# Weight tiles of six groups kept on chip for two blocks of a mixture's first expert

## The chip, the core and the metric

The kernel runs on one core of a Trainium2 chip. A core has TensorE (PE, matrix products into PSUM), VectorE (DVE), ScalarE (ACT) and GpSimd (POOL), which work side by side on SBUF, and SyncE (SP), which here only issues transfers, in order. Each engine works through its own list of instructions in a fixed order and waits where a semaphore isn't reached. The metric is the device time of one execution in microseconds (us).

## What is computed

Three layers follow each other. Each of 32 heads has a recurrent state of 40 x 40 over 768 steps; the 3072 rows of 320 that come out of it go through a PReLU layer of width 2048 (the first expert) and then through a gated SiLU layer of width 1536 (the second expert). All in float32:

```python
for t in range(S):                               # 768 steps
    y[:, :, t] = einsum('bhd,bhde->bhe', r, state)
    Sa = einsum('bhde,bhe->bhd', state, a)
    state = state * w[:, :, None, :] - einsum('bhd,bhe->bhde', Sa, b) \
            + einsum('bhd,bhe->bhde', v, k)
x = y as 3072 x 320
h = x @ w_in                                     # 320 x 2048
x = (maximum(h, 0) + alpha * minimum(h, 0)) @ w_out
g = x @ w_gate                                   # 320 x 1536
return (silu(g) * (x @ w_val)) @ w_out2          # 1536 x 320
```

## The kernel before

**Blocks.** Time is cut into 6 stages m = 0 to 5 (`NM`) of 128 steps. A stage gives 4 x 128 = 512 rows, called block m. The first expert works on block m - 1 while the sequence part (`seq`) works on stage m, so block 4 is worked on beside the last stage, and block 5 after the sequence has ended. The second expert follows, block by block.

**Order.** The program is written as generators that `drive` takes in turn. A scheduler then lists each engine's instructions by priority and by when it expects them to be ready, and assigns the tiles their places; where a tile's place is still held, the first instruction that writes it waits. Nothing is reordered at run time.

**Weights.** Products are made of a high and a low part, so each weight exists as a pair. `conv` converts a raw weight tile into such a pair (`narrow` and `split`): three steps on VectorE (L175 to L177), then on ScalarE, GpSimd or VectorE. The raw tiles have two places (`RB`). The tiles of the first expert (two per group, 384 and 320 KB) and of the second expert's groups 0 to 3 (`KEEP`) are converted early and stored to DRAM as `wd`. The second expert's groups 4 to 11 are converted late, straight into their place in `wpool` (`direct`, 24 tiles).

**First expert** (`mlp1`). The 2048 columns are 16 groups f of 128 (`K1`). For each group `fetch` (L219) brings the up tile from `wd`, 8 matmuls (`up_mm`) give u in PSUM, ScalarE and VectorE make the PReLU (L271, L272) and split it into gh and gl (L187, L188), and 8 matmuls with the group's down tile (`down_mm`) add to three accumulators d0 to d2. So a group is 16 matmuls and 2 fetched tiles. The down product of a group comes behind the up product of the next (`DEP`). Every tile is fetched anew for every block:

```python
def fetch(pool, idx, up):                        # L219
    t = pool.tile([128, 768], F32R, tag="w", name="wt")
    ...
    fetched.append(nc.sync.dma_start(out=..., in_=wd[idx, :, 0:n]))
```

The pool has 4 places (`WB`). u has one PSUM place for blocks 0 to 4 (`psu`) and three for block 5 (`psu3`). At a block's end its accumulators are copied out (x1o) and stored.

**Second expert.** `wpool` has 12 places (`K2`) for each of three kinds of tiles: w0 (gate), w1 (value) and w2 (down). The pool is set up when the sequence's pools are closed and takes their memory. Beside block 5 run the loads of groups 0 to 3 from `wd` (`kept`, L910, 12 tiles, tied by `issue_after` to fetches of block 5) and conversions of groups 4 to 11, one at every fourth step of `mlp1`; the rest run in the second expert's first block. There, for each of 12 groups, 16 matmuls give gate pg and value pv, SiLU and product (L960, L962) make g, and 12 matmuls add to four accumulators.

Of the kernel before, what the change touches and what calls it, by code (L numbers as in the profile page):

```python
# [7 lines left out]
F32 = mybir.dt.float32  # L8
F32R = mybir.dt.float32r
# [3 lines left out]
PSUM = bass.MemoryType.PSUM  # L13
# [34 lines left out]
FA = 8  # L48
# [12 lines left out]
C2 = 10  # L61
GPB = 2
DEP = 1
HELD = 0
XB = 2
L = 64
HALF = 32
LOOK = 2
# [3 lines left out]
def kernel(  # L72
# [16 lines left out]
    NM, B, _, D, NP, TB = r.shape  # L89
# [6 lines left out]
    BLK = B * TB  # L96
    NB = NT // BLK
    K1 = DFF // 128
    K2 = DFF2 // 128
# [56 lines left out]
    mark = {}  # L156
# [58 lines left out]
    fetched = []  # L215
    e1p = {}
    XAB = [XAB1]

    def fetch(pool, idx, up):  # L219
        t = pool.tile([128, 768], F32R, tag="w", name="wt")  # L220
        n = 768 if up else 2 * DM
        fetched.append(nc.sync.dma_start(out=t[:, 0:n].bitcast(F32), in_=wd[idx, :, 0:n]))
        return t.rearrange("p (a b) -> p a b", a=6) if up else t

# [9 lines left out]
    def down_mm(ps, q, t, gh, gl, first, last):  # L234
        if q < 2:
            wh, wl = t[:, q * 128:q * 128 + 128], t[:, 256 + q * 128:384 + q * 128]
            nc.tensor.matmul(ps, wh, gh, start=first, stop=False)
            nc.tensor.matmul(ps, wh, gl, start=False, stop=False)  # L238
            nc.tensor.matmul(ps, wl, gh, start=False, stop=last)  # L239
        else:  # L240
            both = t[:, 512:2 * DM]
            nc.tensor.matmul(ps, both, gh, start=first, stop=False)
            nc.tensor.matmul(ps, both, gl, start=False, stop=last)
# [48 lines left out]
                conv(stage, 2 * K1 + 3 * f + j, src, f, kind)  # L292
                yield

    def mlp1(j, psu, early=0):
        psd, xp1, gp1, wp1 = (e1p[k] for k in ("psd", "xp", "gp", "wp"))
        half = B // 2 * TB
        xs = new_x(xp1, BLK)
        plan = [(f, 0, half) for f in range(early)] + [(f, half, BLK) for f in range(early)]
        plan += [(f, 0, BLK) for f in range(early, K1)]  # L300
        dps = [psd.tile([128, BLK], F32, tag=f"d{q}", name=f"d{q}") for q in range(3)]
        pend = []

        def down(f, c0, c1, gh, gl):
            t = fetch(wp1, 2 * f + 1, False)
            for q in range(3):
                down_mm(dps[q][:, c0:c1], q, t, gh, gl, f == 0 and c0 == 0, f == K1 - 1)

        seen = set()
        for f, c0, c1 in plan:  # L310
            if not seen & {(c0, c1), (0, half) if early and c0 == 0 else (c0, c1)}:
                with lifted():
                    b0, b1 = c0 // TB, c1 // TB
                    fill_x(xp1, xs, xd[j][:, b0:b1].rearrange("f b t -> f (b t)"), c0, c1)
                seen.add((c0, c1))
                yield
            t = fetch(wp1, 2 * f, True)
            ps = psu.tile([128, c1 - c0], F32, tag="u", name="u")
            up_mm(ps, t, tuple(x[..., c0:c1] for x in xs))
            yield  # L320
            if len(pend) == DEP:
                down(*pend.pop(0))
            pend.append((f, c0, c1, *prelu(gp1, ps, f, c1 - c0)))
            yield
        for e in pend:
            down(*e)
        for q in range(3):
            tc.cur_priority -= XPRI
            o = xp1.tile([128, BLK], F32, tag="xa", name="x1o", bufs=XAB[0])
            if q < 2:  # L330
                nc.scalar.copy(out=o, in_=dps[q])
                nc.sync.dma_start(out=x1d[j][q * 128:q * 128 + 128], in_=o)
            else:
                nc.scalar.copy(out=o[lo], in_=dps[2][hi])
                nc.vector.tensor_tensor(out=o[lo], in0=dps[2][lo], in1=o[lo], op=ALU.add)
                mark["x1"] = nc.sync.dma_start(out=x1d[j][256:DM], in_=o[lo])
            tc.cur_priority += XPRI
            yield
# [49 lines left out]
    for j, pool in ((0, rawp), (1, bp)):  # L388
        for nm in ("wa", "bk"):
            t = raw[nm, j] = pool.tile([128, 2, NP, TB], F32, name=f"raw_{nm}{j}")  # L390
# [10 lines left out]
    for j in range(2):  # L401
        if j < NVT or BVT:
            t = (pers if j < NVT else bp).tile([128, NP, TB], F32, name=f"raw_vt{j}")
# [16 lines left out]
    for j in range(2):  # L420
        t = pers.tile([128, NG, L], F32, name=f"tt{j}")
        TT.append(t)
    ST = []
    for j in range(B):
        t = pers.tile([128, NP, 64], F32, name=f"ST{j}")
# [366 lines left out]
    c1, c2 = conv1(), conv2()  # L792
# [38 lines left out]
    c1 = after(mark["prep"], c1)  # L831
    p1, c1 = behind(p1), behind(c1)
    drive((inverse(0), N_INV, HP), (take(p1, EP), EP + .1, BP), (take(c1, EC), EC + .1, CP), lead=1, engs=G0, lag=LG0, who=W0)
    p1, c1 = after(mark["inv"], p1), after(mark["inv"], c1)
# [16 lines left out]
    ps1 = ctx.enter_context(ExitStack())  # L851
    e1 = ctx.enter_context(ExitStack())
    e1p["psd"] = ps1.enter_context(tc.tile_pool(name="psd1", bufs=1, space=PSUM, side="right"))
    psu = ps1.enter_context(tc.tile_pool(name="psu1", bufs=1, space=PSUM, side="right"))
    e1p["xp"] = e1.enter_context(tc.tile_pool(name="xp1", bufs=1, side="right"))
    e1p["gp"] = e1.enter_context(tc.tile_pool(name="gp1", bufs=GPB, side="right"))
    e1p["wp"] = e1.enter_context(tc.tile_pool(name="wp1", bufs=WB, side="right"))
    gms = [mlp1(j, psu, FA if j == 0 else 0) for j in range(NM - 1)]
    if FA:
        drive(  # L860
            (seq(2, 0), N_SEQ, SP), (seq(3, 1), N_SEQ, SP),
# [3 lines left out]
    for m in range(1, NM):  # L865
        s0_ = m * B
        g = [
            (chain(seq(s0_, 0), seq(s0_ + 2, 0)), 2 * N_SEQ, SQ),
            (chain(seq(s0_ + 1, 1), seq(s0_ + 3, 1)), 2 * N_SEQ, SQ),
        ]  # L870
        if m + 1 < NM:
            g.append((chain(preps(range((m + 1) * B, (m + 2) * B)), lift(inverse(m + 1), PV)), FAC * (B * N_PREP + N_INV), HP))
        gm = gms[m - 1]
        nm = N_MLP + (1 if FA and m == 1 else 0)
        held = HELD if m + 1 == NM else 0
        g.append((take(gm, nm - held), nm, 0))
        if not CG:
            g.append((take(c2, CS[m - 1]), CS[m - 1], 0))
        drive(*g, lead=2, engs=G2, lag=LG2, who=W2)
        if CG:  # L880
            for _ in take(after(mark["inv"], c2), CS[m - 1]):
                pass
        assert m + 1 == NM or next(gm, 0) == 0
    ap_.close()
    at.close()
    pa.close()
    cv.close()
    with tc.issue_after(mark["seq"].ins):
        for _ in gm:
            pass  # L890
    XAB[0] = 4
    xp = e1p["xp"] = ctx.enter_context(tc.tile_pool(name="xp", bufs=XB))
    wpool = ctx.enter_context(tc.tile_pool(name="wpool", bufs=K2))
    tail = ctx.enter_context(tc.tile_pool(name="tail", bufs=1))
    wg, wv2, w2 = {}, {}, {}
    KINDS = ((wg, moe2_w_gate, "up"), (wv2, moe2_w_val, "up"), (w2, moe2_w_out, "down2"))
# [15 lines left out]

    c2 = direct()
    with ExitStack() as st:
        psu3 = st.enter_context(tc.tile_pool(name="psu3", bufs=3, space=PSUM))
        gm = mlp1(NM - 1, psu3)
        next(gm)
        xs0 = load_x(xp, x1d[0], BLK)
        for k, _ in enumerate(gm):
            if k % 4 == 2:  # L920
                next(c2, 0)
        last1 = fetched[-2 * K1:]
        for f in range(KEEP):
            with tc.issue_after(last1[LOOK + 5 * f].ins):
                kept(f)
    ps1.close()
    e1.close()
# [98 lines left out]
```

## Time and profile before

| | |
|---|---|
| three runs | 1281.21, 1281.58, 1281.68 us; median 1281.58 us |
| profiled execution | 1281.53 us, of which its span 1279.6 us |
| PE busy | 1099.4 us, 86% of the span |
| VectorE, ScalarE, GpSimd busy | 62%, 46%, 29% |
| sequence's last result stored | about 774 us |
| first product of the second expert | 879.74 us |
| mean granted clock of TensorE | 0.942 |

All times inside an execution count from the start of the span. A chain of waits follows back from the last instruction what each step waited for. "DMA wt<-wd" as the end of a gap means that a weight tile's fetch landed last.

### The profile page before, as it was taken

Reading aid. Unit: us, or ns where it says so; the run is one execution under the profiler, and the core shown is the slowest. Engines: PE = TensorE matmul, PEld = TensorE weight load, DVE = VectorE, ACT = ScalarE, POOL = GpSimd, SP = SyncE. Lnnn points to the kernel's source line nnn. Section 1 sums busy time; section 2 is a strip of 40 time slices with the busy share of each in tenths; the row PEclk is TensorE's granted clock in tenths of the full one; section 3 lists DMA queues with packets and bytes.
Section 4 is the critical chain, followed back from the end, with each engine's and each line's share of the span. In section 5 each row is a group of like instructions: output and inputs, shape, how many; then the busy total and the mean of one; then the engine's idle time right before and its main releaser. Section 6 shows DMA issues by size and latency. Waiting matters only on the chain.

```text
span 1279.6 us, 24549 instructions
## 1 busy us (share of the span) xinstructions
PE 1099.4 (86%) x9056; PEld 928.0 (73%) x9056; DVE 789.7 (62%) x1681; ACT 593.7 (46%) x1463; POOL 374.7 (29%) x566
## 2 busy tenths in 40 slices
PE   3237587888699989999999899989999999999998
PEld 3136466766577778777777686667888888888887
DVE  7898898699848867993876446757532323232222
ACT  4437546754574476468445534535332323232222
POOL 9546565756231224143135301433300000000000
PEclk9657796999799999999999899999999999999999
DMA  5343476775635464554548648896110101000000
GB/s 165 101 149 114 134 228 213 230 235 169 198 110 165 137 184 116 172 177 132 159 132 256 206 126 251 293 337 187 62 46 1 46 1 37 1 16 7 11 11 21
DMA packets 94214, 170.69 MB, mean 133 GB/s; under 512 B 12944, under 2 KB 42896, under 8 KB 94096
## 3 DMA queue, kind: packets, MB, share of 16 engines
q1 hardware_dynamic: 85936, 165.20, 41.1%
q10 hardware_dynamic: 8160, 3.93, 1.1%
q8 instruction: 72, 1.18, 0.4%
q14 instruction: 46, 0.38, 0.1%
HBM read 141.30 MB, written 27.79 MB: 132 GB/s over the span
## 4 chain that ended last, share of the span: by engine, by line
PE 45%; DVE 20%; DMA 11%; ACT 8%; issue 4%; POOL 2%; SPq 1%; ACTq 0%; DVEq 0%; POOLq 0%
PE pg L232 10%; PE pv L232 10%; PE u L232 5%; PE o L947 3%; PE o L946 3%; PE o L948 3%; DVE la L606 3%; DVE tmp L598 3%; DVE g L272 2%; DMA wt<-wd 2%; DMA xd<-pv 2%; DVE wz L176 2%; DMA raw_wa<-in_wa_dram 2%; DVE gs L679 2%; PE gp L735 2%
## 5 line engine op out<-in xcount | busy, mean ns | idle before, releaser
L187 ACT CAST gh<-g 128x512 fp32r<-128x512 f32 (+1 forms) x176 | 105.8, 601 | 179.3 <-DVE g L962 122.3
L962 DVE TENSOR_TENSOR g<-pv,sg 128x512 f32<-128x512 f32 x72 | 49.8, 691 | 215.6 <-PE pv L232 214.4
L232 PE MATMUL u<-xh,wt 128*128 128x512 f32 (+1 forms) x416 | 150.5, 405 | 27.8 <-DVE g L272 20.2
L188 DVE TENSOR_TENSOR gl<-g,gh 128x512 fp32r<-128x512 f32 (+1 forms) x176 | 120.9, 687 | 79.5 <-ACT gh L187 78.2
L272 DVE SCALAR_TENSOR_TENSOR g<-g,neg,u 128x512 f32<-128x512 f32 (+1 forms) x104 | 72.8, 700 | 75.1 <-ACT g L271 74.7
L232 PEld LDWEIGHTS u<-xh,wt 128*128 128x128 f32 x416 | 79.7, 195 | 52.9 <-DVE g L272 27.2
L182 POOL TENSOR_SCALAR wz<-wz 128x384 f32<-128x384 f32 (+1 forms) x56 | 65.8, 1175 | 143.0 <-ACT wz L178 74.2
L960 ACT ACTIVATE sg<-pg 128x512 f32<-128x512 f32 x72 | 42.9, 598 | 133.8 <-PE pg L232 133.8
L232 PE MATMUL pg<-xh,w 128*128 128x512 f32 x288 | 101.9, 394 | 1.4 <-ACT sg L960 1.3
L232 PE MATMUL pv<-xh,w 128*128 128x512 f32 x288 | 100.5, 390 | 0.0
L271 ACT ACTIVATE g<-u 128x512 f32<-128x512 f32 (+1 forms) x104 | 58.7, 565 | 84.9 <-PE u L232 69.2
L537 PE MATMUL mnp<-AN,kbt 128*128 128x128 f32 x384 | 61.9, 314 | 38.4 <-POOL la L585 16.0
L598 DVE TENSOR_TENSOR tmp<-la 128x96 f32<-128x96 f32 (+43 forms) x306 | 87.4, 312 | 3.6 <-POOL la L586 1.6
L947 PE MATMUL o<-w,gh 128*128 128x320 f32 x288 | 87.8, 309 | 0.0
L946 PE MATMUL o<-w,gh 128*128 128x320 f32 x288 | 87.2, 308 | 0.0
L537 PEld LDWEIGHTS mnp<-AN,kbt 128*128 128x128 f32 x384 | 55.5, 222 | 42.3 <-POOL AN L510 19.5
L238 PE MATMUL d<-gl,wt 128*128 128x512 f32 (+1 forms) x208 | 83.0, 401 | 2.5 <-DVE gl L188 2.5
L606 DVE TENSOR_TENSOR la<-la,tmp 128x96 f32<-128x96 f32 (+43 forms) x306 | 82.9, 298 | 2.1
L232 PE MATMUL u<-xl,wt 128*128 128x512 f32 (+1 forms) x208 | 81.3, 391 | 0.6 <-DVE xl L188 0.6
L239 PE MATMUL d<-gh,wt 128*128 128x512 f32 (+1 forms) x208 | 78.6, 380 | 0.0
L693 POOL COPY gs<-raw_v 64x160 f32<-64x160 f32 x96 | 41.4, 432 | 125.6 <-PE yp L750 39.0
L948 PE MATMUL o<-w,gl 128*128 128x320 f32 x288 | 76.7, 308 | 0.0
(118 smaller groups left out, 2706.6 us busy)
## 6 DMA issues: line engine op xcount, KB each, us to landing
wt<-wd SPq DMA_DIRECT2D x104, 384.0 KB
wt<-wd SPq DMA_DIRECT2D x104, 320.0 KB
wd<-wc SPq DMA_DIRECT2D x24, 384.0 KB
raw<-in_moe_w_out_dram SPq DMA_DIRECT2D x28, 320.0 KB
raw_wa<-in_wa_dram SPq DMA_DIRECT2D x48, 160.0 KB
raw_bk<-in_bk_dram SPq DMA_DIRECT2D x48, 160.0 KB
wd<-wc SPq DMA_DIRECT2D x20, 320.0 KB
raw<-in_moe_w_in_dram SPq DMA_DIRECT2D x16, 256.0 KB
```

The source lines that it names most:

```text
L187: nc.scalar.copy(out=h, in_=raw)
L188: eng.tensor_tensor(out=l, in0=raw, in1=h.bitcast(F32), op=ALU.subtract)
L232: nc.tensor.matmul(ps, lt, rh, start=(i == 0), stop=(i == len(ops) - 1))
L238: nc.tensor.matmul(ps, wh, gl, start=False, stop=False)
L239: nc.tensor.matmul(ps, wl, gh, start=False, stop=last)
L272: nc.vector.scalar_tensor_tensor(g, g, neg[:, f:f + 1], ps, ALU.mult, ALU.add)
L537: nc.tensor.matmul(ps[:, s].rearrange("p h t -> p (h t)"), kbt[:, g * SH + s].rearrange("p j t -> p (j t)"), an[:, :, g * SH + s, :],)
L598: nc.vector.tensor_tensor(out=tv, in0=ml[:, kk + 1:HALF, kk:kk + 1].to_broadcast([128, nr, ns]), in1=tl[:, kk:kk + 1, c0:c0 + ns].to_broad ...
L606: mark["inv"] = nc.vector.tensor_tensor(out=dst, in0=dst, in1=tv, op=ALU.subtract)
L946: nc.tensor.matmul(ops[q], gh[:, ts], wh, start=first, stop=False)
L947: nc.tensor.matmul(ops[q], gh[:, ts], wl, start=False, stop=False)
L948: nc.tensor.matmul(ops[q], gl[:, ts], wh, start=False, stop=last)
```

## The change

Three things are changed, with a few that follow from them.

1. `fetch` knows the block. For block 5, and for groups 10 to 15 of block 4 (`HOLD`), it takes a place in `wpool` in place of the four-place pool: up tiles go by turns into w0 and w1, down tiles into w2. Tiles fetched so are remembered in `resident`, and when block 5 wants one that block 4 fetched, it gets that tile and no transfer is issued. Block 5 takes its groups in the order 10 to 15, then 0 to 9.
2. The last 15 steps of block 4 (`held`, six groups and the three results) are written behind the sequence's end, with three PSUM places for u.
3. Beside block 5 a conversion is called at every eighth step (`CTAIL`) where it was every fourth. The loads `kept` are tied to other fetches.

```diff
-HELD = 0
+HOLD = 10
+CTAIL = 8
...
+    resident = {}
+
+    def fetch(pool, idx, up, j):
+        if idx in resident and j == NM - 1:
+            return resident[idx]
         n = 768 if up else 2 * DM
+        if j == NM - 1 or j == NM - 2 and idx >= 2 * HOLD:
+            tag = f"w{idx // 2 % 2}" if up else "w2"
+            t = e1p["hold"].tile([128, n], F32R, tag=tag, name="wt")
+            resident[idx] = t.rearrange("p (a b) -> p a b", a=6) if up else t
+        else:
+            t = pool.tile([128, 768], F32R, tag="w", name="wt")
...
-    def mlp1(j, psu, early=0):
+    def mlp1(j, early=0):
+        fs = [*range(HOLD, K1), *range(HOLD)] if j == NM - 1 else range(K1)
...
-            ps = psu.tile([128, c1 - c0], F32, tag="u", name="u")
+            ps = e1p["psu"].tile([128, c1 - c0], F32, tag="u", name="u")
...
-        held = HELD if m + 1 == NM else 0
+        held = 2 * (K1 - HOLD) + 3 if m + 1 == NM else 0
...
-    with tc.issue_after(mark["seq"].ins):
-        for _ in gm:
-            pass
-    XAB[0] = 4
...
+    wpool = e1p["hold"] = ctx.enter_context(tc.tile_pool(name="wpool", bufs=K2))
...
-        psu3 = st.enter_context(tc.tile_pool(name="psu3", bufs=3, space=PSUM))
-        gm = mlp1(NM - 1, psu3)
+        e1p["psu"] = st.enter_context(tc.tile_pool(name="psu3", bufs=3, space=PSUM))
+        for _ in gm:
+            pass
+        XAB[0] = 4
+        gm = mlp1(NM - 1)
         next(gm)
         xs0 = load_x(xp, x1d[0], BLK)
         for k, _ in enumerate(gm):
-            if k % 4 == 2:
+            if k % CTAIL == 2:
                 next(c2, 0)
-        last1 = fetched[-2 * K1:]
+        last1 = fetched[-2 * HOLD:]
         for f in range(KEEP):
-            with tc.issue_after(last1[LOOK + 5 * f].ins):
+            with tc.issue_after(last1[LOOK + 4 * f].ins):
                 kept(f)
```

Up to the last sequence stage every engine's order is the same in both programs. Lines of the changed kernel are numbered some ten higher. The numbers in names are the tiles'.

**First place.** SyncE's list behind block 5's input (xa from xd). Before: wt_9414 is the down tile of group 8 of block 4, wt_9465 the up tile of group 10; xa is the second expert's first input, raw_ a raw tile to convert.

```order
L222 DMA wt_9414<-wd_69 128x640
L222 DMA wt_9465<-wd_69 128x768
L256 DMA xa_9939<-x1d0_63 128x512
L256 DMA xa_9943<-x1d0_63 128x512
L195 DMA raw_9982<-in_moe2_w_gate_dram 128x2x256
L222 DMA wt_9476<-wd_69 128x640
L260 DMA xa_9947<-x1d0_63 64x512 x2
L222 DMA wt_9505<-wd_69 128x768
L197 DMA raw_9982<-in_moe2_w_gate_dram 64x256 x2
L222 DMA wt_9554<-wd_69 128x640
L195 DMA raw_10053<-in_moe2_w_val_dram 128x2x256
```

Now, from the same tile on (wt_9729 is the up tile of group 10, wt_9740 the down tile of group 9):

```order
L232 DMA wt_9414<-wd_69 128x640
L232 DMA wt_9729<-wd_69 128x768
L232 DMA wt_9740<-wd_69 128x640
L232 DMA wt_9757<-wd_69 128x768
L232 DMA wt_9768<-wd_69 128x640
L232 DMA wt_9785<-wd_69 128x768
L232 DMA wt_9796<-wd_69 128x640
L232 DMA wt_9813<-wd_69 128x768
L232 DMA wt_9824<-wd_69 128x640
L232 DMA wt_9841<-wd_69 128x768
L232 DMA wt_9852<-wd_69 128x640
L232 DMA wt_9869<-wd_69 128x768
```

The fetches for block 4's last groups stand in one run, two more down tiles follow, and the second expert's input and the first raw tile have moved behind them. Block 5 issues 20 fetches in place of 32.

**Second place.** PE's list from the last down product of block 5 (into d2) to the second expert's third gate product. Before, with that third gate product (pg_10766) in the last row:

```order
L243 MATMUL d2_9922<-gl_10499,wt_10502 128x512
L232 MATMUL pg_10687<-xh_9936,w0_10541 128x512
L232 MATMUL pg_10687<-xst_9938,w0_10541 128x512 x2
L232 MATMUL pv_10696<-xh_9936,w1_10543 128x512
L232 MATMUL pv_10696<-xl_9937,w1_10543 128x512
L232 MATMUL pv_10696<-xh_9936,w1_10543 128x512 x2
L232 MATMUL pv_10696<-xl_9937,w1_10543 128x512
L232 MATMUL pv_10696<-xh_9936,w1_10543 128x512
L232 MATMUL pv_10696<-xst_9938,w1_10543 128x512 x2
L232 MATMUL pg_10766<-xh_9936,w0_10547 128x512
```

Now; the row behind the last one here is two matmuls into pv_10618, and then comes the third gate product:

```order
L253 MATMUL d2_9922<-gl_10419,wt_10422 128x512
L242 MATMUL pg_10609<-xh_9936,w0_10463 128x512
L242 MATMUL pg_10609<-xl_9937,w0_10463 128x512
L242 MATMUL pg_10609<-xh_9936,w0_10463 128x512 x2
L242 MATMUL pg_10609<-xl_9937,w0_10463 128x512
L242 MATMUL pg_10609<-xh_9936,w0_10463 128x512
L242 MATMUL pg_10609<-xst_9938,w0_10463 128x512 x2
L242 MATMUL pv_10618<-xh_9936,w1_10465 128x512
L242 MATMUL pv_10618<-xl_9937,w1_10465 128x512
L242 MATMUL pv_10618<-xh_9936,w1_10465 128x512 x2
L242 MATMUL pv_10618<-xl_9937,w1_10465 128x512
L242 MATMUL pv_10618<-xh_9936,w1_10465 128x512
```

The last down product has moved ahead of the whole second pair of products: 16 matmuls stand behind it where 11 stood.

**Third place.** SyncE's list at the first `kept` loads (w0, w1 from wd; raw_ is a raw tile). Before, wt_10111, wt_10135, wt_10152 and wt_10163 are tiles of block 5's groups 4 to 6:

```order
L910 DMA w0_10535<-wd_69 128x768
L910 DMA w0_10541<-wd_69 128x768
L222 DMA wt_10111<-wd_69 128x768
L195 DMA raw_10579<-in_moe2_w_gate_dram 128x2x256
L222 DMA wt_10135<-wd_69 128x640
L910 DMA w1_10537<-wd_69 128x768
L910 DMA w1_10543<-wd_69 128x768
L222 DMA wt_10152<-wd_69 128x768
L197 DMA raw_10579<-in_moe2_w_gate_dram 64x256 x2
L222 DMA wt_10163<-wd_69 128x640
L910 DMA w0_10547<-wd_69 128x768
L910 DMA w1_10549<-wd_69 128x768
```

Now (wt_10307, wt_10349, wt_10377 and wt_10405 are the down tiles of groups 5 to 8):

```order
L917 DMA w0_10457<-wd_69 128x768
L917 DMA w0_10463<-wd_69 128x768
L232 DMA wt_10307<-wd_69 128x640
L232 DMA wt_10349<-wd_69 128x640
L917 DMA w0_10469<-wd_69 128x768
L917 DMA w0_10475<-wd_69 128x768
L232 DMA wt_10377<-wd_69 128x640
L196 DMA raw_10513<-in_moe2_w_gate_dram 128x2x256
L198 DMA raw_10513<-in_moe2_w_gate_dram 64x256 x2
L917 DMA w1_10459<-wd_69 128x768
L232 DMA wt_10405<-wd_69 128x640
L917 DMA w1_10465<-wd_69 128x768
```

The up tiles of block 5 all stand ahead of these loads now, and of its down tiles five stand behind the first of them.


## Rows read from the trace of the kernel before

**Rows 1.** The page: span; busy us (share of the span) xinstructions of each engine

```profile
span 1279.6 us, 24549 instructions
PE 1099.4 (86%) x9056; PEld 928.0 (73%) x9056; DVE 789.7 (62%) x1681; ACT 593.7 (46%) x1463; POOL 374.7 (29%) x566
```

**Rows 2.** Stretches: us, busy (x) of PE, PEld, DVE, ACT, POOL, PEclk, DMA, GB/s

```profile
640.00:776.00 136.00, 125.40 (x1272) 100.64 (x1269) 78.05 (x159) 66.00 (x162) 42.93 (x57) 0.96 0.58 180
776.00:896.00 120.00, 107.05 (x443) 80.85 (x442) 83.36 (x132) 59.23 (x108) 42.00 (x39) 1.00 0.84 273
896.00:1244.00 348.00, 348.00 (x1804) 306.21 (x1803) 106.05 (x157) 96.20 (x169) 9.79 (x9) 1.00 0.07 22
846.00:868.00 22.00, 21.98 (x93) 16.96 (x92) 16.82 (x26) 9.30 (x18) 8.95 (x8) 1.00 0.87 281
832.00:846.00 14.00, 9.81 (x41) 7.10 (x40) 5.93 (x11) 4.95 (x9) 2.34 (x3) 1.00 1.03 375
```

**Rows 3.** Waits of PE from 776 to 896 us: total us, times, longest us

```profile
PE u L232 <- DMA wt<-wd: 5.9, 6, 1.8
PE u L232 <- DVE g L272: 3.8, 4, 1.4
PE d L237 <- DMA wt<-wd: 1.8, 2, 1.6
PE pg L232 <- ACT sg L960: 1.3, 1, 1.3
```

**Rows 4.** Order of time, PE: start, us, operation [idle before <-releaser]

```profile
779.70 0.50 PE L232 MATMUL u<-xh,wt 128*128 128x512 f32 x1 [1.38 <-DVE g L272]
...
879.74 0.50 PE L232 MATMUL pg<-xh,w 128*128 128x512 f32 x1
...
890.55 0.50 PE L232 MATMUL pg<-xh,w 128*128 128x512 f32 x1 [1.34 <-ACT sg L960]
```

**Rows 5.** Transfers from 776 to 880 us: totals, and weight fetches by size

```profile
DMA packets 15732, 30.01 MB, mean 289 GB/s; under 512 B 1776, under 2 KB 6481, under 8 KB 15724
...
wt<-wd SPq DMA_DIRECT2D x22, 384.0 KB
wt<-wd SPq DMA_DIRECT2D x24, 320.0 KB
```

**Rows 6.** Chain of waits from 764 to 900 us: start, us, what

```profile
773.99 3.57 DMA xa<-xd
...
828.70 8.02 DMA wt<-wd
```

**Rows 7.** Order of time, SyncE's queue: start, us, transfer

```profile
775.97 1.06 SPq L222 DMA_DIRECT2D wt<-wd  x2
```

**Rows 8.** Order of time, ScalarE, at the second expert's start

```profile
889.90 1.09 ACT L960 ACTIVATE sg<-pg 128x512 f32<-128x512 f32 x2
```

**Rows 9.** Conversion steps, 776 to 930 us: ns min/median/max, first to last start

```profile
L175 DVE TENSOR_SCALAR wy<-raw x24: 314/359/1046, 789.1 to 911.2; 128x384 uint32<-128x384 uint32 x16, 128x320 uint32<-128x320 uint32 x8
...
L176 DVE SCALAR_TENSOR_TENSOR wz<-raw,wy x24: 493/560/1372, 789.5 to 911.6; 128x384 uint32<-128x384 uint32 x16, 128x320 uint32<-128x320 uint32 x8
...
L177 DVE SCALAR_TENSOR_TENSOR wy<-raw,wz x24: 491/558/1303, 790.6 to 912.1; 128x384 uint32<-128x384 uint32 x16, 128x320 uint32<-128x320 uint32 x8
```

**Rows 10.** Conversion steps grouped, 776 to 896 us: busy us, mean ns

```profile
L176 DVE SCALAR_TENSOR_TENSOR wz<-raw,wy 128x384 uint32<-128x384 uint32 (+1 forms) x20 | 16.0, 798 | 0.6
...
L177 DVE SCALAR_TENSOR_TENSOR wy<-raw,wz 128x384 uint32<-128x384 uint32 (+1 forms) x20 | 14.2, 709 | 0.5
...
L175 DVE TENSOR_SCALAR wy<-raw 128x384 uint32<-128x384 uint32 (+1 forms) x20 | 8.3, 413 | 7.4 <-DMA raw<-in_moe_w_val_dram 3.0 <-POOL wz L183 2.5 <-DMA raw<-in_moe_w_gate_dram 1.5
```

**Rows 11.** Order of time, GpSimd: the last conversion's last step

```profile
914.96 0.88 POOL L188 TENSOR_TENSOR w<-wz,w 128x320 fp32r<-128x320 f32 x1 [2.02 <-ACT w L187]
```

**Rows 12.** Order of time, VectorE, two groups of the second expert

```profile
923.47 0.69 DVE L962 TENSOR_TENSOR g<-pv,sg 128x512 f32<-128x512 f32 x1 [3.35 <-PE pv L232]
...
928.89 0.69 DVE L962 TENSOR_TENSOR g<-pv,sg 128x512 f32<-128x512 f32 x1 [3.35 <-PE pv L232]
```

More of the change, by code (lines that the diff above doesn't have):

```diff
@@ L217 @@
     XAB = [XAB1]
-    def fetch(pool, idx, up):
-        t = pool.tile([128, 768], F32R, tag="w", name="wt")
+    resident = {}
+    def fetch(pool, idx, up, j):
+        if idx in resident and j == NM - 1:
+            return resident[idx]
         n = 768 if up else 2 * DM
+        if j == NM - 1 or j == NM - 2 and idx >= 2 * HOLD:
[4 more added lines that the diff above has]
+            t = pool.tile([128, 768], F32R, tag="w", name="wt")
         fetched.append(nc.sync.dma_start(out=t[:, 0:n].bitcast(F32), in_=wd[idx, :, 0:n]))
@@ L299, in mlp1 @@
         plan = [(f, 0, half) for f in range(early)] + [(f, half, BLK) for f in range(early)]
-        plan += [(f, 0, BLK) for f in range(early, K1)]
+        plan += [(f, 0, BLK) for f in fs if f >= early]
         dps = [psd.tile([128, BLK], F32, tag=f"d{q}", name=f"d{q}") for q in range(3)]
@@ L304, in down @@
         def down(f, c0, c1, gh, gl):
-            t = fetch(wp1, 2 * f + 1, False)
+            t = fetch(wp1, 2 * f + 1, False, j)
             for q in range(3):
-                down_mm(dps[q][:, c0:c1], q, t, gh, gl, f == 0 and c0 == 0, f == K1 - 1)
+                down_mm(dps[q][:, c0:c1], q, t, gh, gl, f == fs[0] and c0 == 0, f == fs[-1])
         seen = set()
@@ L316, in mlp1 @@
                 yield
-            t = fetch(wp1, 2 * f, True)
-            ps = psu.tile([128, c1 - c0], F32, tag="u", name="u")
+            t = fetch(wp1, 2 * f, True, j)
+            ps = e1p["psu"].tile([128, c1 - c0], F32, tag="u", name="u")
             up_mm(ps, t, tuple(x[..., c0:c1] for x in xs))
@@ L853 @@
     e1p["psd"] = ps1.enter_context(tc.tile_pool(name="psd1", bufs=1, space=PSUM, side="right"))
-    psu = ps1.enter_context(tc.tile_pool(name="psu1", bufs=1, space=PSUM, side="right"))
+    e1p["psu"] = ps1.enter_context(tc.tile_pool(name="psu1", bufs=1, space=PSUM, side="right"))
     e1p["xp"] = e1.enter_context(tc.tile_pool(name="xp1", bufs=1, side="right"))
@@ L857 @@
     e1p["wp"] = e1.enter_context(tc.tile_pool(name="wp1", bufs=WB, side="right"))
-    gms = [mlp1(j, psu, FA if j == 0 else 0) for j in range(NM - 1)]
+    gms = [mlp1(j, FA if j == 0 else 0) for j in range(NM - 1)]
     if FA:
@@ L882 @@
                 pass
-        assert m + 1 == NM or next(gm, 0) == 0
+        assert held or next(gm, 0) == 0
     ap_.close()
@@ L887 @@
     cv.close()
-    with tc.issue_after(mark["seq"].ins):
-        for _ in gm:
-            pass
-    XAB[0] = 4
     xp = e1p["xp"] = ctx.enter_context(tc.tile_pool(name="xp", bufs=XB))
-    wpool = ctx.enter_context(tc.tile_pool(name="wpool", bufs=K2))
+    wpool = e1p["hold"] = ctx.enter_context(tc.tile_pool(name="wpool", bufs=K2))
     tail = ctx.enter_context(tc.tile_pool(name="tail", bufs=1))
```

## The prediction

> **What bounds the kernel now.** I read the share of the engines first [rows 1]: TensorE (PE) is busy for 1099 of the 1280 us, no other engine for more than 62%. The table by stretches [rows 2] says where PE's idle time lies. From 896 us to 1244 us, the second expert, PE is busy for all 348 us and nothing can be won there. From 640 to 776 us, with the last sequence stages, it is idle for 10.6 us, which belongs to the sequence's own chain. Between them, from 776 to 896 us, the last part of the first expert, PE is busy for 107.05 of 120 us: 12.95 us idle. The granted clock is 1.00 there, the 2.4 GHz level, so a gap costs its length and nothing more.
>
> The list of PE's waits in that stretch [rows 3] names who ends the gaps: weight tiles from DRAM 5.9 + 1.8 = 7.7 us in 8 gaps, VectorE's PReLU 3.8 us in 4, ScalarE's first SiLU 1.3 us in one. The order of time [rows 4] places the two outer ones: the first VectorE gap ends at 779.70 us (1.38 us), the SiLU gap at 890.55 us, behind the second expert's first product at 879.74. The list of transfers [rows 5] has the cause of the 7.7 us in it: 46 weight tiles in 104 us, on DMA engines that move 289 GB/s on the mean, through a pool of four places (two groups ahead), behind transfers for the second expert in the same in-order queue. One of these fetches took 8.02 us on the chain [rows 6].
>
> That PE can run this stage without gaps the profile shows too [rows 2]: from 846 to 868 us it is busy for 21.98 of 22 us, 93 matmuls, or 22 / 93 x 16 = 3.79 us for a group of 16, with VectorE at 16.82 of 22 us and conversions going on beside it. So once the weights are there, VectorE's load at 76% does not hold PE up.
>
> **The change part by part.** All times are of the profiled execution: 1281.53 us, of which 1279.6 are the span; the median of the timed runs is 1281.58.
>
> *Twelve fetches go.* Groups 10 to 15 of block 4 are fetched into the second expert's places and read again, first, by block 5. That takes 6 x (384 + 320) KB = 4.3 MB of the stretch's 30.0 MB away [rows 5]. Block 5 starts with six groups, 6 x 3.79 = 22.7 us, that need no fetch at all.
>
> *The other fetches go far ahead.* SyncE's order shows the held fetches as one run behind block 5's input, with no raw weight between them (order, first place). Block 5's input, which waits for the sequence's last store, is fetched from 773.99 us [rows 6], and SyncE issues the tile before the first held one at 775.97 us [rows 7]; the sequence's memory, which the held tiles take, is free by then. A group's 704 KB needs 0.721 MB / 289 GB/s = 2.5 us of DMA against 3.79 us of PE, so supply runs away from demand. The critical tile is the first, group 10's up tile. PE wants it some 2.6 us behind 779.70, at 782.3 us. In front of it stand block 5's input (768 KB) and one tile (320 KB): 1472 KB, 1.51 MB, at 289 GB/s from 773.99 us [rows 6] gives 779.2 us. Bounds: nothing, or, with the longest landing of 8.02 us from about 776.5, 784.5, a wait of 2.2 us. I take nothing, since the nearest row, the input's landing of 3.57 us, is short. So the 7.7 us of weight waits go.
>
> *Three PSUM places for the up products from group 10 of block 4 on*, where there was one until block 5. PE no longer waits for group f's PReLU before it starts f + 1. Group 9 still uses the single place, so the 1.38 us at 779.70 stay; 3.8 - 1.4 = 2.4 us go.
>
> *The start of the second expert.* Between the last down product and the third gate product, which waits for the first SiLU, PE had 11 matmuls of work and now has 16 (order, second place), 5 x 21.98 / 93 = 1.2 us more. ScalarE still copies out three results and then runs the SiLU, started at 889.90 [rows 8]. Of 1.3 us some 0.3 stay: 1.0 us goes. Bounds: 0 to 1.3.
>
> *Conversions move back.* Before, 20 of the second expert's 24 directly converted tiles have been begun by 896 us [rows 9, 10]; by VectorE's order 7 stand behind the last PReLU, now 12. VectorE works as much as before in all, and PE has no gap there. The price hangs on pace. The 24 conversions run from 789.5 to 911.6 us by their second VectorE step [rows 9]: 122.1 / 23 = 5.31 us each. Now they start behind the PReLU of group 14 of block 4: 779.7 + 5 x 3.79, 1.9 us for its up product and some 2.5 us for the PReLU, about 803 us. The 22nd, the gate tile of group 11, begins at 803 + 21 x 5.31 = 914.5 us and is done 914.96 + 0.88 - 911.6 = 4.2 us later [rows 9, 11], at 918.7. PE wants it at the new start of the second expert, 879.7 [rows 4] - 10.1 = 869.6 us, plus 1.8 us of the last down product and 11 groups of 928.89 - 923.47 = 5.42 us [rows 12]: 931.0 us. So 12 us are left and the cost is nothing; from 5.9 us a conversion on it would cost. Since conversions stand between the products on VectorE in a fixed order, I charge 1.0 us for hand-overs here and at block 5's start (bounds 0 and 5.4, one group).
>
> The port is the one thing that could spoil this pace. The second and third VectorE step of a conversion take 0.56 us at the median and 1.37 and 1.30 us at most [rows 9]: two prices for one instruction. The Trainium skill ("SBUF — State Buffer", Who interferes with whom) says that a VectorE instruction with two SBUF inputs and a GpSimd instruction that reads SBUF shut each other out for a whole instruction. The trace agrees in the two prices. By that rule a conversion's length depends on what GpSimd happens to run beside it, and the worst case is a rival below.
>
> Sum: 7.7 + 2.4 + 1.0 - 1.0 = 10.1 us. 1281.5 - 10.1 = 1271.4 us.
>
> **Rivals.** *The kept loads are the cause.* The worst stretch is 832 to 846 us, 9.81 us of PE in 14 [rows 2], while twelve tiles for the second expert's groups 0 to 3 are loaded at 375 GB/s. Those loads stay. If they still hit fetches that are due, the 4.2 us of that stretch come back: 1275.6 us. For it: 375 is well above the mean of 289. Against: with the first kept load only five of block 5's tiles are unfetched, the down tiles of groups 5 to 9, while PE works on the held groups (order, third place).
>
> *VectorE takes the place of the fetches.* Block 5's PReLUs share VectorE with conversions; if each weight gap was covering a late PReLU, the 7.7 us are given back and only 2.4 remain: 1279.1 us. For it: VectorE ends 4 of the 13 gaps [rows 3]. Against: the gapless 22 us above, and fewer conversions per group now.
>
> *Slower: the conversions become the bound of the second expert's first block.* If VectorE and GpSimd collide on nearly every step, the three VectorE steps go from their means (0.413, 0.798, 0.709) to their longest (1.046, 1.372, 1.303) [rows 9, 10]: 1.80 us more each, 7.11 us a conversion. The 22nd is done at 803 + 21 x 7.11 + 4.2 = 956.5 us, 25.5 us late: 1271.4 + 25.5 = 1296.9 us. From 5.9 us on it costs, from 5.9 + 10.1 / 21 = 6.4 us on the kernel is slower than before. For it: more conversions wait for a raw tile with only two raw places. Against: the mean pace has been 5.31 with 12 more fetches around.
>
> *It doesn't do what it says*: a held place is overwritten and fetched again. SyncE's order has 12 fetches fewer, so this is nearly excluded; 1281.5 us.
>
> **How the numbers follow.** The forecast holds with 0.70; its own range is 1269.3 (all but 0.7 of the 12.95 us gone) to 1275. Kept loads 0.14 at 1275.6, VectorE 0.08 at 1279.1, conversions 0.06 at 1297, no effect 0.02 at 1281.5. The range from 1269.3 to 1278.5 takes in the first two and leaves out some 0.16. A measurement of this kernel can tell about 0.2% (2.6 us) from no change, so faster means under 1279.0: 0.70 + 0.14 + half of 0.08 = 0.88. Same: 0.04 + 0.02 = 0.06. Slower: 0.06.
>
> **What would show it.** Right: between 776 us and the second expert's first product, PE's waits name no weight tile, only about 1.4 us of PReLU; SyncE's fetches stand some 20 us ahead of their use; PE has no gap in the second expert; its first product starts near 869 us. Wrong: a gap at the first held tile near 782 us (released too late), gaps behind a weight tile near the kept loads, gaps by PReLU in block 5, or SiLU and weight casts that PE waits for in groups 8 to 11 of the second expert's first block.

## The result and the profile after

The changed kernel took 1264.71, 1259.99 and 1266.84 us in timed runs and 1269.55 us in the profiled execution: median 1265.78 us against 1281.39 us for the kernel before, so the medians lie 15.6 us apart. The ratio of the means is 0.9884 with a 95% interval of 0.9837 to 0.993: 14.9 us faster (9 to 21). The forecast was 10.1 us faster, 1271.4 us, in a range from 1269.3 to 1278.5. The direction and the places were right; the gain was half as large again, and the median lies below the range. The profiled execution alone would lie inside it, and that is luck: the part ahead of the changed places came out 2.6 us longer in it, as shown below.

The waits are read first. PE's waits in the profile of the changed kernel, from 776 to 896 us (total us, times, longest us; before: [rows 3]):

```profile
PE u L242 <- DVE g L282: 1.4, 1, 1.4
PE u L242 <- DMA wt<-wd: 1.1, 1, 1.1
PE pg L242 <- ACT sg L970: 0.6, 1, 0.6
```

Of eight weight waits one is left, of four PReLU waits one, and half of the SiLU wait: 3.1 us in place of 12.8. The order of time has their places (before: [rows 4]):

```profile
782.32 0.50 PE L242 MATMUL u<-xh,wt 128*128 128x512 f32 x1 [1.41 <-DVE g L282]
...
786.17 0.47 PE L242 MATMUL u<-xh,wt 128*128 128x512 f32 x1 [1.06 <-DMA wt<-wd]
...
868.92 0.40 PE L242 MATMUL pg<-xh,w 128*128 128x512 f32 x1
...
878.90 0.50 PE L242 MATMUL pg<-xh,w 128*128 128x512 f32 x1 [0.65 <-ACT sg L970]
```

The stretches answer to [rows 2]:

```profile
776.00:896.00 120.00, 116.88 (x518) 95.07 (x517) 81.24 (x128) 59.63 (x108) 35.63 (x34) 1.00 0.71 239
832.00:846.00 14.00, 14.00 (x62) 11.33 (x61) 9.60 (x17) 6.76 (x12) 5.21 (x5) 1.00 0.99 361
896.00:1244.00 348.00, 348.00 (x1802) 306.08 (x1801) 111.40 (x167) 99.55 (x176) 16.11 (x15) 1.00 0.07 22
```

In the 14 us in which PE lost most before, it has no gap now, with transfers at 361 GB/s beside it. In the same 120 us it does 518 matmuls in place of 443.

To compare the two executions, a stretch with the same work in it is needed: from the first up product behind the PReLU wait (779.70 us before, 782.32 after) to the second expert's third gate product (890.55 and 878.90). It has 408 matmuls in both; below it is called *the stretch*, what lies ahead of it *the head*. Its row before, then after:

```profile
779.70:890.55 110.85, 99.28 (x408) 74.75 (x409) 76.56 (x121) 53.25 (x98) 40.99 (x38) 1.00 0.84 275
```

```profile
782.32:878.90 96.58, 94.87 (x408) 76.39 (x409) 64.28 (x103) 47.95 (x86) 29.16 (x27) 1.00 0.73 251
```

The stretch is 14.27 us shorter. Only 9.86 us of that are idle time that went (110.85 - 99.28 = 11.57 against 96.58 - 94.87 = 1.71). The other 4.41 us are *busy* time that went, for the same matmuls at the same granted clock of 1.00. The profiled execution is accounted for with this: 1281.53 - 14.27 from the stretch, + 2.62 because the head came out longer in this execution, - 0.33 behind the stretch and around the span, is 1269.55 us. So two things are to be explained: busy time that vanishes, and a head that varies while PE's order in it is the same.

Theory A: a wait costs PE more than its idle row. The row calls a matmul busy for some 0.39 us, but with a full pipeline one starts every 0.23 us. Behind a wait this overlap is missing. The order of time of the kernel before shows it at the wait that was priced at 1.38 us:

```profile
777.70 0.39 PE L239 MATMUL d<-gh,wt 128*128 128x512 f32 x1
777.93 0.39 PE L243 MATMUL d<-gl,wt 128*128 128x512 f32 x1
779.70 0.50 PE L232 MATMUL u<-xh,wt 128*128 128x512 f32 x1 [1.38 <-DVE g L272]
780.04 0.40 PE L232 MATMUL u<-xl,wt 128*128 128x512 f32 x1
780.27 0.39 PE L232 MATMUL u<-xh,wt 128*128 128x512 f32 x1
```

The starts are 0.23 us apart, then 1.77, 0.34 and 0.23. The wait cost 1.77 + 0.34 - 2 x 0.23 = 1.65 us, 0.27 more than its row. And a wait shorter than 0.16 us (0.39 - 0.23) is no idle time at all. Over the stretch, 39 intervals between starts are longer than 0.26 us before, with 16.5 us in excess of the pace; after there are 4, with 2.2 us. The difference is the 14.3 us. The intervals also say what the rows before leave out, 16.5 - 11.6 = 4.9 us: 1.92 us are overlap lost ahead of the twelve waits with a row of over 0.1 us, 1.22 us are slower second starts behind such waits, and 1.77 us stand in 15 intervals at waits too short for a row. After the change the same three are 0.5 us, and 4.9 - 0.5 are the 4.4 us of busy time.

Rivals: the busy time or the stretch as a whole differs between executions (B), or another part of the change, conversions moved back (F), gave what the forecast did not count. The expectations name more: C (the depth of the fetches), D (their volume), E (a gap costs its row and no more, the prediction's own step), G (depth and reuse stand in for each other), H (conversions do not matter), I (another wait takes the place of the one taken out).

### The profile page after: what moved, and what is told of

The parts are those of the page before. It is cut to its first block, busy times and chain, and to the rows that moved or that the text cites. A ratio compares the mean times of both kernels' runs of the same rounds, so it can differ in the third digit from the quotient of the medians.

```text
span 1267.8 us, 24534 instructions
## 1 busy us (share of the span) xinstructions
PE 1097.0 (87%) x9056; PEld 931.9 (74%) x9056; DVE 789.1 (62%) x1681; ACT 593.8 (47%) x1463; POOL 376.4 (30%) x566
## 4 chain that ended last, share of the span: by engine, by line
PE 51%; DVE 25%; ACT 9%; DMA 8%; issue 4%; POOL 2%; SPq 1%; ACTq 0%; DVEq 0%; POOLq 0%
PE pg L242 10%; PE pv L242 10%; PE u L242 7%; DVE tmp L609 4%; DVE la L617 4%; PE o L957 3%; PE o L956 3%; PE o L958 3%; DVE AN L523 2%; DMA raw_vt<-in_vt_dram 2%; DMA raw_wa<-in_wa_dram 2%; DVE g L282 2%; PE d L247 2%; DMA xd<-pv 2%; PE d L248 2%
## 5 line engine op out<-in xcount | busy, mean ns | idle before, releaser
L242 PE MATMUL u<-xh,wt 128*128 128x512 f32 (+1 forms) x416 | 147.9, 397 | 19.9 <-DVE g L282 18.6
L548 PE MATMUL mnp<-AN,kbt 128*128 128x128 f32 x384 | 64.8, 324 | 39.1 <-POOL raw_vt L416 17.1
L548 PEld LDWEIGHTS mnp<-AN,kbt 128*128 128x128 f32 x384 | 58.5, 233 | 42.9 <-POOL raw_vt L416 17.1
```

Source lines behind the costliest of these rows:

```text
L242: nc.tensor.matmul(ps, lt, rh, start=(i == 0), stop=(i == len(ops) - 1))
L548: nc.tensor.matmul(ps[:, s].rearrange("p h t -> p (h t)"), kbt[:, g * SH + s].rearrange("p j t -> p (j t)"), an[:, :, g * SH + s, :],)
```

## The experiments

A table of all thirteen traced executions with this stretch (the twelfth experiment alters its start). "Idle" is its length less PE's busy time; "1.2 GHz" is what matmuls at that clock cost in it (last section), worked out from their starts at the pace of 0.231 us; busy is net of that.

| kernel | stretch, us | idle | busy, net | 1.2 GHz | ratio to before (95%) |
|---|---|---|---|---|---|
| before | 110.85 | 11.57 | 99.28 | | |
| before, again (e7) | 109.87 | 11.26 | 98.61 | | 0.9988 (0.9968 to 1.0008) |
| before, conversions back (e10) | 112.47 | 11.31 | 98.5 | 2.7 | 0.9991 (0.9968 to 1.0014) |
| before, three u places (e5) | 107.32 | 7.53 | 98.2 | 1.6 | 0.9983 (0.997 to 0.9996) |
| four places, refetch (e9) | 103.76 | 5.33 | 96.9 | 1.6 | 0.9945 (0.9926 to 0.9964) |
| the same, conversions every 4th (e11) | 103.57 | 4.90 | 97.4 | 1.3 | 0.993 (0.9907 to 0.9954) |
| reuse, four places (e6) | 101.11 | 3.69 | 95.9 | 1.6 | 0.9925 (0.9907 to 0.9943) |
| one u place (e4) | 100.35 | 2.22 | 96.6 | 1.6 | 0.9923 (0.9905 to 0.9941) |
| group 10 not held (e8) | 98.30 | 2.32 | 96.0 | | 0.99 (0.9883 to 0.9917) |
| conversions every 4th (e3) | 97.66 | 2.68 | 95.0 | | 0.9898 (0.9879 to 0.9916) |
| no reuse (e2) | 96.79 | 1.40 | 95.4 | | 0.9907 (0.9892 to 0.9921) |
| changed | 96.58 | 1.71 | 94.9 | | 0.9884 (0.9837 to 0.993) |
| changed, again (e1) | 95.00 | 0.22 | 94.8 | | 0.989 (0.9873 to 0.9908) |

### e1: the changed kernel again

No edit.

> The changed kernel, unaltered, run again. Theory A (pauses): what the change is worth lies in one stretch, from the first up product behind the PReLU wait of block 4's group 9 (779.70 us before, 782.32 us after) to the second expert's third gate product: 408 matmuls in 110.85 us before and in 96.58 us after. That stretch is 96.6 us again, within 0.5, and what spreads the times (1260 to 1270 us) lies ahead of it, where both programs have the same order: there the head will be shorter or longer than 782.3 by some us, with another pattern of 1.2 GHz windows. Rival B (luck of the transfers): the stretch itself differs by several us between executions, and the head does not. Time: 1262 to 1268 us by A.

```profile
784.20:879.20 95.00, 94.78 (x409) 76.47 (x409) 64.11 (x103) 48.34 (x87) 29.09 (x27) 1.00 0.74 256
```

Median 1264.70 us, ratio 0.989 (0.9873 to 0.9908). The stretch was 1.6 us shorter than in the first execution, more than the 0.5 expected, because the waits for the first held tile and for the SiLU were nearly gone in this one. The head was longer: 784.20 us. So the stretch differs by 1 to 2 us between executions, not by the 14 of the change, and the spread of the times lies mostly ahead of it. This row also is the measure of a stretch without waits: 94.78 us of work for 408 matmuls, 0.232 us each.

### e7: the kernel before again

No edit.

> The kernel before, unaltered, in another execution. Theory A: the stretch of 408 matmuls is 110.85 us again within 1 us, PE's waits in it sum to 11 to 12 us of idle rows and PE's busy time is 98 to 100 us for the same matmuls; the head ahead of it is between 775 and 784.2 us, as in the ten executions traced so far. Rival B (luck of the transfers): the stretch differs by several us.

```profile
783.98:893.85 109.87, 98.61 (x408) 75.11 (x408) 76.19 (x121) 52.94 (x97) 41.34 (x38) 1.00 0.84 276
```

109.87 us with 11.26 us idle: the high busy time (98.61) is there again, and rival B has no support. The mean over two executions each is 110.4 against 95.8 us, 14.6 us apart; the ratios of the times give 14.1 and 14.9.

### e4: one PSUM place for u

```diff
-        e1p["psu"] = st.enter_context(tc.tile_pool(name="psu3", bufs=3, space=PSUM))
+        e1p["psu"] = st.enter_context(tc.tile_pool(name="psu3", bufs=1, space=PSUM))
```

> The change with one PSUM place for u behind the sequence, where it has three: a kernel with many short PReLU waits at known places, and weights as in the changed kernel. About 21 waits of 1.4 us of idle row each, as the one at 782.32. Theory A (a wait costs more than its idle row: 1.77 us from start to start around the 1.38 us at 779.70, where 0.23 is the pace, and 0.11 more for the first matmul behind it): 1.65 us each, so the stretch grows by 21 x 1.65 = 35 us while PE's idle rows in it grow by 29, and PE's busy time for the same 408 matmuls rises from 94.9 to about 100 us. Rival E (a gap costs its idle row and nothing more, the step of the prediction): busy time stays at 94.9 us. Time by A about 1300 us.

Median 1270.61 us, ratio 0.9923. The expectation missed its number: I had taken one wait for each group, and PE waited three times for a PReLU in the stretch, since the down products of the group before cover most of it. So this was no test of 21 waits. What it has: 2.22 us of idle rows, and a stretch 3.8 us longer than the changed kernel's, 1.6 of them from matmuls at 1.2 GHz. The three places are worth some 2 to 4 us, near the 2.4 forecast for them.

### e2: fetched again, but far ahead

```diff
         if idx in resident and j == NM - 1:
-            return resident[idx]
+            pass
```

> The change without the reuse: block 5 fetches groups 10 to 15 again, into the second expert's places, so that SyncE issues 32 fetches for block 5 as before. Theory C (depth): what matters is that the fetches run far ahead, not how many there are; the stretch of 408 matmuls stays within 2 us of 96.6 and the time is within 3 us of the changed kernel. Rival D (volume): 12 fetches of 4.3 MB at 289 GB/s are 15 us of transfers in a stretch of 104 us that they fill to nine tenths; weight waits come back, at least half of the 7.7 us of before, and the stretch is 101 us or longer.

```profile
777.45:874.24 96.79, 95.39 (x409) 76.23 (x409) 60.83 (x96) 45.86 (x82) 24.29 (x23) 1.00 0.80 285
```

Median 1268.47 us, ratio 0.9907, against 0.989 for the changed kernel run beside it (1264.70 us). The time is thus 2 to 4 us longer, where at most 3 were expected, and the stretch has only a part of it. All 12 transfers are back, the DMA engines are at 0.80 in place of 0.73, and the stretch is 96.79 us: 0.2 longer than in one execution of the changed kernel, 1.8 than in the other. Rival D is refuted: fewer transfers are not what ended the weight waits. That they were issued far ahead is enough.

### e6 and e9: back to four places, with and without the reuse

```diff
-        if j == NM - 1 or j == NM - 2 and idx >= 2 * HOLD:
+        if j == NM - 2 and idx >= 2 * HOLD:
```

e6 is this edit; e9 is this and that of e2.

> The change with the reuse, but block 5's other 20 fetches go through the old pool of four places. Theory C (depth): two groups ahead is too little beside the loads for the second expert, so weight waits come back behind the six held groups, 2 to 5 us of idle rows, and each such wait costs some 0.3 us more than its idle row; the stretch is 99 to 103 us. Rival D (volume): 12 fetches fewer are what ended the waits; with them gone four places do, and the stretch stays within 1 us of 96.6.

> The changed kernel without the reuse and with block 5's 32 fetches in the pool of four places: of the fetches only block 4's last six groups still go far ahead. Theory G (depth and reuse stand in for each other): alone each cost little when it was taken away, together they are the weight waits of before; 4 to 7 us of idle rows by weight tiles in block 5, and the stretch is 104 to 108 us. Rival F (the conversions moved back and the three u places did most): the stretch stays under 102 us.

PE's waits from 776 to 896 us, e6 and then e9:

```profile
PE u L242 <- DVE g L282: 2.5, 2, 1.9
PE pg L242 <- ACT sg L970: 1.8, 1, 1.8
PE u L242 <- DMA wt<-wd: 1.1, 2, 0.9
PE pg L242 <- DVE g L282: 0.2, 1, 0.2
```

```profile
PE u L242 <- DMA wt<-wd: 2.3, 4, 0.9
PE pg L242 <- ACT sg L970: 1.8, 1, 1.8
PE d L247 <- DMA wt<-wd: 1.0, 1, 1.0
PE pg L242 <- DVE g L282: 0.2, 1, 0.2
```

With the reuse, four places give two weight waits back (1.1 us; I had expected 2 to 5), without it five (3.3 us). Net of matmuls at 1.2 GHz the stretch is 99.5 and 102.2 us. So depth alone took 102.2 to 96.8 (5.4 us), the reuse alone 102.2 to 99.5 (2.7 us), and beside depth the reuse adds 0.2 to 1.8 us. They stand in for each other, as theory G said, though e9 missed its numbers: a stretch just below the 104 us and 3.3 us of weight waits where 4 to 7 were expected.

### e3, e10 and e11: the conversions

e3 is the changed kernel with `CTAIL = 4`; e11 is e9 with that; e10 is the kernel before with

```diff
-            if k % 4 == 2:
+            if k % 8 == 2:
```

> The changed kernel with conversions called at every fourth step again (CTAIL 4), all else as changed. Theory C (depth): with the fetches far ahead the extra raw tiles do no harm and VectorE has room; the stretch of 408 matmuls stays at 95 to 98 us. Rival F (the conversions moved back are a good part of the gain, since they leave VectorE and the queue to block 5): PReLU and weight waits come back and the stretch is 100 us or longer. From the measured parts: taking away depth alone made it 101.1 us (99.5 without the 1.6 us that a 1.2 GHz window cost there), three u places 100.4 (98.8), the reuse 96.8, against 95.0 and 96.6 with all; these add up to no more than half of the 14.3 us, so a part is still unplaced and F would place it.

> The kernel before with one thing of the change: conversions called at every eighth step beside block 5 (k % 8). Weights, pool and PSUM places stay. Theory F (with four places each raw transfer in the queue delays a fetch, so moving conversions back gives weight waits back to PE): the stretch goes from 110.85 to 103 to 107 us. Rival H (the conversions do not matter, as at the changed kernel, where calling them twice as often moved the stretch by 1 to 3 us): 109 us or more.

> The changed kernel without the reuse, with block 5's 32 fetches in the pool of four places, and conversions at every fourth step: of the change remain the three u places and the held fetches of block 4's last six groups. Against 103.76 us for the same kernel with conversions at every eighth step (102.1 without the 1.6 us that a 1.2 GHz window cost there): by theory F 106 to 110 us, near the 107.3 us of the kernel before with three u places; by rival H 102 to 104 us.

e10's stretch, and the part of it at 1.2 GHz:

```profile
784.30:896.77 112.47, 101.16 (x409) 77.23 (x409) 71.57 (x112) 49.87 (x91) 33.98 (x31) 0.97 0.81 263
...
823.76:829.86 6.10, 6.10 (x14) 4.81 (x15) 2.74 (x5) 1.61 (x3) 1.15 (x1) 0.50 0.84 295
```

Conversions at every eighth step alone: ratio 0.9991 (0.9968 to 1.0014), 109.8 us net of those matmuls, as before. e11 against e9: 102.3 and 102.2. e3 against the changed kernel: 97.66 against 96.58 and 95.00, and 0.9898 against 0.9884 in time. Rival F is refuted in all three pairs; what is left for it is 1 to 3 us in e3, from a PReLU and a SiLU wait.

### e5: three u places in the kernel before

```diff
-HELD = 0
+HELD = 15
...
-        psu3 = st.enter_context(tc.tile_pool(name="psu3", bufs=3, space=PSUM))
-        gm = mlp1(NM - 1, psu3)
+        e1p["psu"] = st.enter_context(tc.tile_pool(name="psu3", bufs=3, space=PSUM))
+        for _ in gm:
+            pass
+        XAB[0] = 4
+        gm = mlp1(NM - 1)
```

> The kernel before with one thing of the change: the last 15 steps of block 4 stand behind the sequence with three PSUM places for u; no held tiles, no reuse, conversions at every fourth step. The PReLU waits in block 4 go (2.4 us of idle rows before), but the weights arrive no sooner. Theory A with depth: weight waits take a part of them over, and the stretch goes from 110.85 to 108 to 111 us. Rival: the whole 2.4 us and their pauses go, 107 us or less.

Ratio 0.9983 (0.997 to 0.9996), 2.2 us (0.5 to 3.8) faster. The stretch is 107.32 us, 105.7 net of matmuls at 1.2 GHz, with weight waits of 3.9 + 1.5 us left of 7.7. The gain in the stretch is 3.5 us (5.1 net), above the 0 to 3 expected; net it lies where the rival had it (107 us or less), so weight waits did not take the place of the PReLU waits.

### e8 and e12: the two waits that are left

e8 leaves group 10 in the old pool, so that the first held tile is wanted one group later. e12 opens the three u places one group sooner:

```diff
-        if j == NM - 1 or j == NM - 2 and idx >= 2 * HOLD:
+        if j == NM - 1 or j == NM - 2 and idx >= 2 * HOLD + 2:
...
-        held = 2 * (K1 - HOLD) + 3 if m + 1 == NM else 0
+        held = 2 * (K1 - HOLD) + 5 if m + 1 == NM else 0
```

(the first pair is e8, with block 5's order and `last1` moved by the one group; the second is e12)

> The changed kernel with group 10 of block 4 left in the four-place pool, and groups 11 to 15 held and reused (10 fetches fewer than before in place of 12); three u places from group 10 as changed. The first held tile is then wanted one group later. If the 1.06 us wait at 786.17 us for the first held tile is the price of the place that comes free only when the sequence's memory does, it goes, and the stretch is 95.0 us, as in the execution of the changed kernel that had no such wait. If it is the queue behind block 5's input that holds it, the wait stays or moves to the four-place tile: 96 to 97 us. Time 1263 to 1268 us either way.

> The changed kernel with the three u places from group 9 of block 4 on, one group sooner; held tiles and reuse as changed. The PReLU wait that stands at the start of the stretch in every execution (1.38 us of idle row at 779.70 before, 1.41 at 782.32 after; 1.77 and 1.8 us from start to start) goes. From the sequence's last matmul to the second expert's third gate product it was 105.8 us (changed kernel) and 104.2 us (the same, again). Theory A (a wait costs its start interval less the pace, and the slower second start): 1.54 + 0.11 = 1.65 us go, so 102.5 to 104.2. Rival E (a gap costs its idle row): 1.4 us. Rival I: the wait for the first held tile, one group behind it, takes its place: 104 to 106 us. A gain this small is not seen in the times; the trace decides.

e8: ratio 0.99, stretch 98.30 us. The held tile's wait went, and in its place stand smaller ones for the four-place tile, a longer SiLU wait (1.9 us) and a VectorE wait: no gain, and above both values expected (95.0, or 96 to 97). So e8 doesn't tell whether the place or the queue held that tile. e12: ratio 0.9888 (0.9869 to 0.9906), from the sequence's last matmul to the third gate product 104.06 us (105.77 and 104.22 for the changed kernel); at the edge between theory A and rival I, it decides nothing between the two prices of a wait. The PReLU wait is gone, and one step later stands

```profile
781.78 0.72 PE L247 MATMUL d<-gh,wt 128*128 128x512 f32 x2 [1.12 <-ACT gh L188]
```

ScalarE's order of time says why:

```profile
778.23 0.62 ACT L188 CAST xh<-xa 128x512 fp32r<-128x512 f32 x1 [2.73 <-DMA xa<-xd]
778.76 0.59 ACT L281 ACTIVATE g<-u 128x512 f32<-128x512 f32 x1
779.39 0.62 ACT L188 CAST xh<-xa 128x512 fp32r<-128x512 f32 x1
780.59 0.62 ACT L271 CAST xst<-xa 128x512 fp32r<-128x512 f32 x1 [0.58 <-DMA xa<-xd]
781.11 0.61 ACT L188 CAST gh<-g 128x512 fp32r<-128x512 f32 x1
```

The cast gh for block 4 is listed behind the three casts that take in block 5's input, and the third of them waits for its transfer. In the changed kernel the activation that the PReLU needs stands behind the first of these casts:

```profile
780.26 0.62 ACT L188 CAST xh<-xa 128x512 fp32r<-128x512 f32 x1 [2.69 <-DMA xa<-xd]
780.79 0.59 ACT L281 ACTIVATE g<-u 128x512 f32<-128x512 f32 x1
```

So a wait for block 5's input is what PE sees here, wherever the three u places begin. Neither of the two beats the changed kernel.

## Why the prediction was wrong, point by point

- **The step that failed: "so a gap costs its length and nothing more".** The forecast added up idle rows, 7.7 + 2.4 + 1.0 us, and the lower end of the range was set by "all but 0.7 of the 12.95 us gone". The rows hold less than the waits cost. In the stretch the idle rows sum to 11.57 us and the intervals between starts to 16.5 us in excess of the pace, in 39 places; after the change 1.71 and 2.2. That is 14.3 us where the rows show 9.9. In the table busy time rises with idle time in nearly every line, from 94.8 us at 0.22 us idle to 99.28 at 11.57.

  It could have been read before: [rows 2] have 93 matmuls in 22 gapless us, 0.2366 us each; 408 of them are 96.5 us, and 110.85 - 96.5 = 14.3. That this hits the measured 14.3 is luck: short waits raise the pace in those 22 us, by 2.2 us over 408 matmuls, and 2.2 us of waits happen to stay after the change. With the other terms the sum closes: of the 11.1 us of idle rows that were to go 9.9 went, the 1.0 us for hand-overs was not paid, and 4.4 us went that no row held, 14.3 in all.

  The Trainium skill warns of the measure ("Perfetto Trace Analysis", Identifying the Most-Contended Engine): matmuls are pipelined, so their busy share says little about the headroom, and the share of the peak arithmetic and the busy share of the weight loads are to be taken in its place. The trace agrees for the weight loads: PEld is busy for 74.75 of 110.85 us before and 76.39 of 96.58 after, so what it isn't busy for falls from 36.1 to 20.2 us, by 15.9, nearer to the 14.3 than the 9.9 of the matmul rows. The prediction didn't weigh it.
- **Weight waits, -7.7 us: right but for 1.1.** One of 1.06 us is left, at the tile for which the prediction had the bounds 0 to 2.2 and took nothing. The chain shows it landing at 785.93, later than either end (779.2, 784.5) if the 2.6 us of this execution's later head are not added:

```profile
779.25 6.68 DMA wt<-wd
```

- **The cause of it, only half right.** I gave 4.3 MB fewer transfers a paragraph of its own. e2 shows that they matter little once fetches run ahead; e6 and e9 that they are worth 2.7 us where they don't. What counts more is how far ahead the fetches are issued; SyncE's run of 14 behind block 5's input is a part of that:

```profile
778.56 11.08 SPq L232 DMA_DIRECT2D wt<-wd  x14
```

  Net of matmuls at 1.2 GHz the runs make a ladder: a stretch of 110.4 us before (mean of two), 105.7 with three u places (e5), 102.3 with the held fetches as well (e11; 102.2 in e9), 96.8 with block 5's fetches deep too (e2), 95.8 with the reuse (mean of two). That is 4.7, 3.4, 5.5 and 1.0 us. Single executions differ by 1 to 2 us, and from e5 to e11 the order of block 5's groups and the moment of the kept loads change too, which no run took by itself.

- **Three u places, -2.4 us: right in place, a little low.** The 1.4 us at the first group stayed as forecast (1.41). Alone, before the change, they gave 2.2 us of time and 3.5 to 5 us of the stretch (e5); taken away from the changed kernel they cost 2 to 4 us of it (e4).
- **SiLU, 0.3 us to stay:** 0.65 in one execution, 0.2 in the other; right within that.
- **Conversions, no cost: right.** They were to start at about 803 us and keep 5.31 us. The steps of the changed kernel (ns min/median/max, first to last start; before: [rows 9]):

```profile
L177 DVE SCALAR_TENSOR_TENSOR wz<-raw,wy x24: 493/559/1214, 802.4 to 923.1; 128x384 uint32<-128x384 uint32 x16, 128x320 uint32<-128x320 uint32 x8
```

  (923.1 - 802.4) / 23 = 5.25 us each, and PE has no gap from 896 to 1244 us. The 1.0 us charged for hand-overs was not found: behind the SiLU wait it takes the same time to the end of the span, 389.08 and 389.04 us before (the second in e7), 388.91 and 388.86 us after (the second in e1). The two prices of a step do go with GpSimd, as the prediction said: of the 48 second and third steps before the change 16 took over 0.65 us, each with a GpSimd instruction beside it, and of the 32 shorter ones 8 had one.
- **The rivals.** Kept loads: refuted; SyncE issued the twelve from 825.0 to 850.6 us (822.8 to 845.9 before), and 832 to 846 us are gapless. VectorE in the place of the fetches: no PReLU wait is left in block 5. Conversions as the bound: refuted by their pace. No effect: refuted.
- **The head.** Over 13 traced executions it was 775.0 to 784.3 us, with the same order on PE. The forecast took one profiled execution for the kernel, which spreads by 9 us from this alone; the profiled execution of the changed kernel (1269.55) was the longest of its four. What sets the head is not settled: its differences build up along the sequence, and the time at 1.2 GHz in it explains them in part only (from 105 us on, 80 to 98 us, with a correlation of 0.5 over the 13).

What no experiment shows by itself is the price of one kind of wait: the split of the 4.4 us is read from the start times of two executions, and e4, which was to multiply one kind of wait, didn't make enough of them. Open too are the head, and which of the place and the queue delayed the first held tile.

## What to carry to other kernels

Price a stretch with gaps by its length less the number of its matmuls times the pace of a gapless stretch, not by the sum of its idle rows; here the rows held 11.6 of 16.5 us. Where fetches are waited for, try a deeper pool before fewer transfers: issued far ahead, 12 transfers more cost next to nothing. And before taking out the last small wait, look at what stands behind it on the engine that ends it, since here each one taken out showed the next.

## What had not been expected of the hardware

Waits of over 2 us were sometimes followed by a stretch at 1.2 GHz in the midst of the work. All waits are given here from start to start. In e10 one took 2.78 us (an idle row of 2.39):

```profile
820.98 0.40 PE L239 MATMUL d<-gh,wt 128*128 128x512 f32 x1
823.76 0.80 PE L232 MATMUL u<-xh,wt 128*128 128x512 f32 x1 [2.39 <-DMA wt<-wd]
824.36 0.63 PE L232 MATMUL u<-xl,wt 128*128 128x512 f32 x1
```

From there to 829.86 us the granted clock is 0.50 in the row of e10 above, and 14 matmuls take 6.10 us, where 14 x 0.232 = 3.2 us would be their time. In e4, e5, e6 and e9 nine matmuls cost 1.6 us more, within 2 us behind the wait at the head's end (2.2 to 2.3 us from start to start there); in e11 it followed a wait of 2.49 us in block 5. The waits of 1.7 to 2.1 us at the head's end (before, changed, e1, e2, e3, e7, e8, e10, e11) were followed by none. But none followed a wait of 2.23 us in the kernel before (up to 836.76 us) or one of 2.63 us in e7 either, so the length of the wait alone does not decide it.
